# Transposes joined to values, score runs of a whole pair, and seven block products in two more MLP steps

## The chip, the cores and the metric

The kernel runs on one NeuronCore of a Trainium2 chip. The metric is device time in microseconds for one launch. A NeuronCore has a matmul engine (TensorE, PE in the profile, with its weight loads shown apart as PEld), VectorE (DVE), ScalarE (ACT), GpSimd (POOL) and a queue engine for transfers (SP). Matmul results land in PSUM, whose banks the kernel deals out by tags: two for `sc`, one each for `tr` and `xa`, and four shared ones.

## The reference

Two stages. The first is attention in chunks: batch 4, 8 heads, 768 rows, head size 64; each chunk of 32 rows sees 8 memory rows, its own 32 rows, 16 to the left and 8 to the right. The second takes the result as x (4 x 768 x 512), adds the real part of its 2D Fourier transform, normalizes rows, and adds a two-layer MLP.

```python
for c in range(nc):
    k_ctx, v_ctx = k[:, :, l_start:r_end], v[:, :, l_start:r_end]
    k_full = np.concatenate([mem_k, k_ctx], axis=2)
    v_full = np.concatenate([mem_v, v_ctx], axis=2)
    scores = scale * np.matmul(q_c, k_full.transpose(0, 1, 3, 2))
    a = softmax(scores)
    out[:, :, c_start:c_end] = np.matmul(a, v_full)
...
mixed = np.real(np.fft.fft(np.fft.fft(x, axis=1), axis=2))
u = x + mixed
un = (u - mu) / np.sqrt(var + 1e-06)
out = u + np.maximum(un @ w_ch1, 0.0) @ w_ch2
```

## The kernel before

**Attention.** Heads go in pairs, four pairs a batch, 16 pairs `n` in all (0 to 15). For pairs 0 to 11 q and k are loaded in natural order by POOL's queue (`e_load_qk`, three buffers each) and transposed by 16 small matmuls each (`e_turn_q` into the one PSUM bank of tag `tr`; `e_turn_k` into a shared bank for pairs 0 to 3, into `tr` for 4 to 11). ACT copies them out (`e_qT`, L423; `e_kT`, L448, by DVE for the first four pairs). For batch 3 (pairs 12 to 15) SP's DMA transposes do it instead. `e_scores` (L461) makes the scores of half a pair (12 matmuls of 64x64, six tiles of 64 rows for two heads) in the two banks of tag `sc`; `e_exp` (L469) takes them through exp on ACT in two instructions into one of three `e1` buffers; then the other half follows in the same two banks. From pair 4 on `e_values` (L485) runs for both halves in a row, 24 matmuls into the bank `xa` and 24 into a shared bank named `xo`. `e_norm` on DVE divides and writes to `xsb`.

**Fourier.** For each batch DVE folds the rows (`zy`, `pq`, `ff`, `lo`), ACT makes the upper halves of split numbers, PE multiplies with cosine and sine tables (`ps` L557, `pm` L727 and L608), DVE adds to `xsb` and takes statistics (L741, L742). Half of the mirrored rows comes back through DRAM (`x_rows`, `x_back`).

**MLP.** A batch has three steps `(b, j)` of 256 rows. `e_un` makes the normalized rows on ACT: in batches 0 and 1 it subtracts the mean alone, with the sign turned and `rstd` applied at the end; in batches 2 and 3 (the set `EVEN`) it applies scale and mean together, from `e_scale` on POOL. SP transposes them (`e_flip`, L776) into `unT`. Layer 1, `e_ch1` (L803): eight groups of 8 matmuls of 256 columns into a shared bank `ph`, each followed by a relu on ACT (L812) into `hT`. Layer 2 in batches 0 and 1: `e_ch2` (L821), 32 matmuls of 512 columns, and `e_res` (L828) on DVE. In the steps of the list `FAST`, so far those of batches 2 and 3, layer 2 is a 2 x 2 block product with seven block multiplications instead of eight: `e_prod` (L870), 56 matmuls of 256 columns; DVE prepares sums of the blocks of `hT` (`e_s`, L858) and adds the products to `xsb` (`e_add`, L875). The sums of weight blocks are made once (`e_w2t`, L845: four DVE instructions, the last of which overwrites a block of `w_sb` and so comes after the last plain layer 2).

**Shared banks.** Two banks of tag `acc` and two of tag `mlp`. `ph`, `pc`, `ps`, `pm` and `xo` live there; a task with a `pick` takes whichever of the four has been free longest.

**Order.** The order of all instructions on all engines is written out by a planner (`Plan`) when the kernel is built. Every task has an engine, a cost in microseconds, tasks it comes after, slots it takes and gives back, and a rank. `order` plays the list through in time: on each engine the task of lowest rank that is ready goes next; MLP matmuls have high ranks and fill PE's time between attention and Fourier tasks. `shortest` does this 24 times with the ranks of the later tasks shifted at random, and emits the order whose modelled end is earliest. The chip then runs each engine's queue in that order, with semaphores between engines.

Of the kernel before, what the change touches and what calls it, by code (L numbers as in the profile page):

```python
# [37 lines left out]
class Plan:  # L38
# [18 lines left out]
    def add(self, engine, cost, emit, after=(), take=(), give=(), rank=None, moved=0.0,  # L57
            loose=False, late=0.0, filler=False, behind=None, lag=0.0, pick=None, grain=0.1, head=1.0):
        t = dict(engine=engine, cost=cost, emit=emit, after=[a for a in after if a is not None],
                 take=take, give=give, rank=len(self.tasks) if rank is None else rank,  # L60
                 moved=moved, done=None, at=None, no=len(self.tasks), loose=loose,
                 late=late, filler=filler, behind=behind, lag=lag, pick=pick, grain=grain, head=head)
        self.tasks.append(t)
        return t
# [31 lines left out]
    def shortest(self, tries, spread):  # L96

        free, ranks = dict(self.free), [t["rank"] for t in self.tasks]
        found = None
        for i in list(range(tries)) + [None]:  # L100
            draw = random.Random(found[1] if i is None else i)
            even = (found[1] if i is None else i) == 0
            self.free = dict(free)
            for t, rank in zip(self.tasks, ranks):
                move = draw.gauss(0.0, spread)
                t["rank"] = rank if even or rank < self.lead or rank > 1e5 else rank + move
                t["done"] = t["at"] = None
                if t["pick"] is not None:
                    t["pick"].pop("tag", None)
            placed = self.order()  # L110
            if found is None or self.end < found[0]:
                found = (self.end, i)
        return placed

    def order(self):
# [9 lines left out]
        while any(waiting.values()):  # L125
# [5 lines left out]
            for e, ts_ in waiting.items():  # L131
# [3 lines left out]
                for t in ts_:  # L135
# [12 lines left out]
                    take = t["take"]  # L148
                    if t["pick"] is not None:
                        take += tuple(sorted((x for x in t["pick"]["of"] if self.free[x] > 0),  # L150
                                             key=lambda x: (since.get(x, []) + [0.0])[0]
                                             + t["pick"]["of"].index(x) * 0.5))[:1] or ("",)
                    for tag in take:
# [8 lines left out]
                    if t["pick"] is not None:  # L162
                        t["pick"]["tag"] = take[-1]
                    cost = t["cost"] * (2.0 if e == "PE" and now < self.WARM else 1.0)
# [41 lines left out]
def kernel(  # L206
# [15 lines left out]
    P = 128  # L222
# [217 lines left out]
    def e_kT(n, eng=None):  # L440
        if n >= TURNED * HP:
            win = LEFT + 64 + RIGHT
            nc.vector.tensor_copy(
                strided(kTb[n % NKT], MEM0 + NMEM, [[P, NT], [1, win]]),
                strided(kU[n % NKU], KR - LEFT, [[64, NT], [1, win]]))
            return
        trk = tr_of.pop((n, 1))
        (eng or nc.scalar.copy)(  # L448
            strided(kTb[n % NKT], MEM0 + NMEM, [[P, NT], [RB, 11], [1, RB]]),
            strided(trk, 0, [[64 // RB, NT], [1, 11], [KP, RB]]))  # L450
        if n < HP:
            let_go(trk)
# [284 lines left out]
    def e_stats(b, kt):  # L737
# [4 lines left out]
        nc.vector.bn_aggr(mu_of[b][:, kt, :], st6)  # L742

    def e_un(b, kt):
        un_of[b, kt] = un = fpool.tile([P, DM], FP16, tag="un", bufs=6, name="un")

        if b not in EVEN:
# [58 lines left out]
    def e_relu(b, j, i):  # L806
        if i == 0:
            shape = [P, 2, HH, 2 * P]
            hT_of[b, j] = (wpool.tile(shape, FP16, tag="w2t", bufs=1, name="hT") if (b, j) == (0, 1) else
                           fpool.tile(shape, FP16, tag="hT", bufs=1, name="hT"))  # L810
        ph = ph_of.pop((b, j, i))
        nc.scalar.activation(hT_of[b, j][:, :, i, :], ph, AFT.Relu, bias=0.0,  # L812
                             scale=1.0 if b in EVEN else -1.0)
        let_go(ph)
# [9 lines left out]
    def e_res(b, j, r):  # L824
        u, pc = xs[b][:, slot(b, 2 * j + r), :], pc_of.pop((b, j, r))
        st = slot(b, 2 * j + r)
        if b not in EVEN:
# [140 lines left out]

    t_used = {}

    def attention(n):
# [27 lines left out]
        else:  # L999
            tq = add("PE", 0.46, lambda: e_turn_q(n), [lq, t_idb], take=("tr",), give=("qs",))  # L1000
# [4 lines left out]
            tk = add("PE", 0.48, lambda: e_turn_k(n), [lk, t_idb, t_kz if n == 0 else t_kzs],  # L1005
                     take=(ktag,), give=("ks",))
            ek = add(dve[0], 1.25 if dve[1] else 1.04, lambda: e_kT(n, dve[1]), [tk, mk],
                     give=(ktag,))
        t_used[0, at], t_used[1, at] = (eq, tk) if b >= TURNED else (tq, tk)
        xs_ = []  # L1010
        for g in range(2):
            s_ = add("PE", 0.30, lambda g=g: e_scores(n, g), [eq, ek], take=("sc",),
                     give=("qT", "kTb") if g == 1 else (),
                     behind=t_sc.get((n, 0)))
            t_used["kTb", n % NKT] = s_
            t_sc[n, g] = s_
            t_exp[n, g] = x_ = add("ACT", 1.05, lambda g=g: e_exp(n, g),
                     [s_, t_masks, t_after.get(n)], take=("e1",), give=("sc",))
            xs_.append(x_)
# [191 lines left out]
    def columns_of(b, t_rest):  # L1211
# [31 lines left out]

        t_sum = {}
        columns(kts[0])
        for i, kt in enumerate(kts):
# [12 lines left out]
            sa = add("DVE", 0.9, lambda kt=kt: e_stats(b, kt), [su, sa])  # L1259
            if b in EVEN:  # L1260
                if i % 2:
                    t0, t1 = kts[i - 1], kt
                    sc_ = add("POOL", 1.7, lambda t0=t0, t1=t1: e_scale(b, t0, t1 - t0), [sa])
                    for t in (t0, t1):
                        un = add("ACT", 0.78, lambda t=t: e_un(b, t), [sc_], take=("un",))
                        t_un[t] = add("SP", 1.2, lambda t=t: e_flip(b, t), [un],
                                      behind=t_un.get(kts[kts.index(t) - 1]) if t else None,
                                      take=room(t), give=("un",), late=2.5, loose=True)
                continue
            un = add("ACT", 0.78, lambda kt=kt: e_un(b, kt), [sa], take=("un",))  # L1270
            if b > 0:
                t_un[kt] = add("SP", 1.2, lambda kt=kt: e_flip(b, kt), [un],
                               behind=t_un.get(kts[i - 1]) if i else None,
                               take=room(kt), give=("un",), late=2.5, loose=True)
# [4 lines left out]
                           take=room(kt), give=("mlp",))  # L1279
        return t_un, add("POOL", 2.05, lambda: e_rstd(b), [sa]) if b not in EVEN else None  # L1280

# [165 lines left out]
```

## Time and profile before

| | us |
|---|---|
| median of 3 runs | 280.53 (280.51 to 280.87) |
| the profiled execution | 280.87 |
| its span, first to last instruction | 279.2 |
| PE: starts of score runs, 32 of 12 matmuls | 13.0 to 182.5 |
| values of pairs 4 to 15 start at | 51.5, 59.7, 70.0, 81.4, 85.9, 90.9, 105.5, 112.2, 147.5, 152.8, 174.4, 185.5 |
| layer 1 of (1,0), (1,1), (1,2) starts at | 127.05, 151.8, 168.3 |
| last matmul starts | 275.7 |

A page of the profile covers one execution. Busy time of an engine is the union of its instructions. Matmuls overlap in their records, so how long a run of them holds TensorE is read from the distance between the start of the run and the start of the next. `x12` counts instructions merged into one line; `128*64 128x65` are weights and moving data. The granted TensorE clock is 1.00 in all stretches.

### The profile page before, as it was taken

What the parts mean: (1) busy time and instruction counts of PE and PEld (TensorE: products, weight loads), DVE (VectorE), ACT (ScalarE), POOL (GpSimd) and SP (SyncE); (2) the same over time, 40 slices, a digit from 0 to 9 for tenths busy, and PEclk for the clock granted to TensorE, in tenths of its full rate; (3) what the DMA queues carried; (4) which work ended last, traced back from release to release, by engine and by line L of the source; (5) the groups of instructions that cost most, each with busy time, mean ns of one, the idle gap of its engine ahead of it and who ended that gap; (6) DMA issues with size and microseconds to landing.
All of it is one profiled execution on the core that took longest, in us unless ns stands there. A gap on an engine that the chain in (4) does not pass through costs nothing.

```text
span 279.2 us, 7959 instructions
## 1 busy us (share of the span) xinstructions
PE 264.8 (95%) x3318; PEld 208.3 (75%) x3318; DVE 192.6 (69%) x424; ACT 154.7 (55%) x262; POOL 63.5 (23%) x127
## 2 busy tenths in 40 slices
PE   0599999999999999999999999999999999999995
PEld 0387797888765668758767857668889888888884
DVE  7968999941238999999937851259987975353444
ACT  6888647788777527636653556328164191605150
POOL 8852572330201096050211130001100130000000
PEclk9999999999999999999999999999999999999999
DMA  5998999999998999979992586824842057303152
GB/s 95 209 177 159 184 191 203 196 198 194 197 198 216 122 226 165 139 193 156 268 162 78 109 137 178 152 78 137 98 183 40 0 96 149 97 38 77 54 100 76
DMA packets 116116, 39.98 MB, mean 143 GB/s; under 512 B 104560, under 2 KB 111472, under 8 KB 116080
## 3 DMA queue, kind: packets, MB, share of 16 engines
q1 hardware_dynamic: 93888, 23.54, 45.6%
q0 software_dynamic: 21472, 15.21, 33.3%
q10 hardware_dynamic: 720, 0.72, 0.7%
q8 instruction: 26, 0.43, 0.7%
q14 instruction: 10, 0.08, 0.1%
HBM read 37.36 MB, written 13.37 MB: 182 GB/s over the span
## 4 chain that ended last, share of the span: by engine, by line
PE 82%; DVE 6%; POOL 5%; DMA 2%; ACT 2%; issue 2%; POOLq 0%; DVEq 0%
PE ph L803 26%; PE pc L821 15%; PE pc L870 11%; PE ps L557 6%; PE pm L727 5%; PE xa L485 4%; PE xo L485 4%; PE ps L716 3%; PE sc L461 3%; DMA qs<-in_q_dram 2%; PE trq L405 2%; PE trk L405 1%; PE idle L930 1%; ACT un L752 1%; PE pm L608 1%
## 5 line engine op out<-in xcount | busy, mean ns | idle before, releaser
L803 PE MATMUL ph<-unT,w_sb 128*128 128x256 f16 x768 | 90.0, 273 | 0.2 <-ACT hT L812 0.2
L812 ACT ACTIVATE hT<-ph 128x512 f16<-128x512 f32 x96 | 56.8, 597 | 47.3 <-PE ph L803 27.5
L803 PEld LDWEIGHTS <-w_sb 128*128 128x128 f16 x768 | 73.6, 98 | 10.8 <-issue 0.8
L821 PE MATMUL pc<-w_sb,hT 128*128 128x512 f16 x192 | 44.7, 380 | 0.0
L469 ACT ACTIVATE e<-sc,mbias 128x384 f32<-128x384 f32 x64 | 33.6, 580 | 17.7 <-PE sc L461 17.7
L821 PEld LDWEIGHTS <-hT 128*128 128x128 f16 x192 | 17.6, 98 | 19.2 <-issue 0.2
L870 PEld LDWEIGHTS <-hT 128*128 128x128 f16 x240 | 23.3, 98 | 3.9 <-issue 1.0
L875 DVE TENSOR_TENSOR xsb<-pc,xsb 128x256 f32<-128x256 f32 x43 | 17.8, 420 | 9.6 <-PE pc L870 8.4
L870 PE MATMUL pc<-w_sb,hT 128*128 128x256 f16 x192 | 24.1, 273 | 0.2 <-DVE xsb L875 0.2
L828 DVE SCALAR_TENSOR_TENSOR xsb<-pc,rstd,xsb 128x512 f32<-128x512 f32 x12 | 9.0, 749 | 18.8 <-PE pc L821 18.8
L569 ACT CAST up<-ps 128x386 f16<-128x386 f32 x16 | 9.7, 603 | 21.4 <-PE ps L557 20.4
L741 DVE BATCH_NORM_STATS2 st<-xsb 128x6 f32<-128x512 f32 x24 | 16.5, 687 | 0.5
L858 DVE TENSOR_TENSOR S<-hT 128x768 f16<-128x768 f16 (+1 forms) x12 | 5.1, 424 | 16.4 <-ACT hT L812 15.8
L485 PEld LDWEIGHTS xa<-va,e 128*64 128x64 f32 x384 | 13.1, 143 | 3.6 <-issue 2.9
L485 PE MATMUL xa<-va,e 128*64 128x65 f32 x384 | 15.4, 232 | 0.0
L752 ACT ACTIVATE un<-xsb,rs 128x512 f16<-128x512 f32 x12 | 9.5, 807 | 10.1 <-POOL rs L767 10.1
L485 PE MATMUL xo<-va,e 128*64 128x65 f32 x384 | 14.5, 227 | 0.0
L461 PEld LDWEIGHTS <-kTb 64*128 64x128 bf16 x384 | 7.7, 97 | 8.0 <-issue 5.3
L485 PEld LDWEIGHTS xo<-va,e 128*64 128x64 f32 x384 | 13.0, 142 | 0.4 <-ACT ff L651 0.3
L542 ACT CAST hi<-ff 128x768 f16<-128x768 f32 x12 | 9.9, 830 | 4.9 <-DVE ff L534 4.7
L461 PE MATMUL sc<-qT,kTb 64*128 64x64 bf16 x384 | 11.6, 196 | 0.9 <-POOL va L345 0.9
L870 PE MATMUL pc<-w_t,S 128*128 128x256 f16 x96 | 11.6, 272 | 0.4 <-DVE xsb L875 0.4
(168 smaller groups left out, 442.3 us busy)
## 6 DMA issues: line engine op xcount, KB each, us to landing
va<-in_v_dram SPq DMA_DIRECT2D x32, 220.0 KB
w_sb<-in_moe_w_ch_dram POOLq DMA_DIRECT2D x8, 512.0 KB, 14.5
out_dram<-xsb SPq DMA_DIRECT2D x12, 256.0 KB
qs<-in_q_dram POOLq DMA_DIRECT2D x12, 192.0 KB, 6.7
ks<-in_k_dram POOLq DMA_DIRECT2D x12, 192.0 KB, 6.7
x_rows<-xsb POOLq DMA_DIRECT2D x3, 768.0 KB, 4.6
xr<-x_back POOLq DMA_DIRECT2D x3, 768.0 KB, 6.0
out_rows<-xsb SPq DMA_DIRECT2D x9, 256.0 KB
```

The source lines that it names most:

```text
L461: nc.tensor.matmul(sc[:, hh, t6, :], kT[r0:r0 + 64, t, :], qT[r0:r0 + 64, ts(t, 64)], start=True, stop=True, tile_position=(r0, 0))
L469: nc.scalar.activation(e1[:, :, :, ts(half, 32)], sc[:, :, 0:6, ts(half, 32)], AFT.Exp, bias=mbias[:, half:half + 1], scale=1.0 / math.sqr ...
L485: nc.tensor.matmul(xa[64 * half:64 * half + 64, st, hh, 0:65], e1[:, hh, t6, :], v1[:, hh, 6 * g + t6, 0:65], start=True, stop=True)
L557: nc.tensor.matmul(out_[:, sp, :], part[:, ab, sp * 3 + st, c0:c1], tab[:, sp, st, :], start=(st == 0 and i == 0), stop=(st == 2 and i == 1))
L727: nc.tensor.matmul(pm[:, par, :], lhs, rhs[:, par, :], start=(im == 0), stop=(im == 3))
L741: nc.vector.bn_stats(st6, xs[b][:, kt, :])
L752: nc.scalar.activation(un, xs[b][:, kt, :], AFT.Identity, bias=rs[:, 1:2], scale=rs[:, 0:1])
L803: nc.tensor.matmul(ph[:, k, :], w1_sb[:, dt, ts(HH * k + i, P)], unT_of[b, j][:, dt, :], start=(dt == 0), stop=(dt == NDT - 1))
L812: nc.scalar.activation(hT_of[b, j][:, :, i, :], ph, AFT.Relu, bias=0.0, scale=1.0 if b in EVEN else -1.0)
L821: nc.tensor.matmul(pc_of[b, j, r], hT_of[b, j][:, k, i, ts(r, P)], w2_sb[:, HH * k + i, :], start=(i + k == 0), stop=(i + k == HH))
L870: nc.tensor.matmul(pc_of[key], a[:, i, :], w[:, i, :], start=(i == 0 and new), stop=(i == HH - 1), skip_group_check=not new)
L875: nc.vector.tensor_tensor(u, pc, u, ALU.add)
```

## The change

Four things, and the planner's costs that go with them.

1. A task can take more than one shared bank: `pick` becomes a list, `picks`.
2. `FAST` also holds (1, 1) and (1, 2). Tiles 1, 2, 4, 5 of batch 1 are therefore normalized with scale and mean together, in the two groups (1, 4) and (2, 5); tiles 0 and 3, of (1, 0), stay as they were. The sums of weight blocks now come after (1, 0).
3. For pairs 6 to 11 (`JOINED`) both transposes of pair n are emitted in the task of the values of pair n - 2, behind them; that task comes after the loads of pair n too, and takes `tr` for q and one more shared bank for k.
4. For pairs 8 to 15 all 24 score matmuls run in a row (`a_scores`), after the values of pair n - 1. The first six tiles go to `sc`, the other six to `tr` and to a shared bank, one for each head. `a_exp` takes the first half through exp in two instructions and the second in four.

The costs of single transposes, half score runs and values in the planner rise from 0.46, 0.48, 0.30 and 1.5 to 0.56, 0.56, 0.37 and 1.64; two transposes behind values add 0.81, and a run of a whole pair costs 0.52.

```diff
-    FAST = [(b, j) for b in range(2, B) for j in range(3)]
-    EVEN = {b for b, j in FAST}
+    FAST = [(1, 1), (1, 2)] + [(b, j) for b in range(2, B) for j in range(3)]
+    MIXED = 1
+    JOINED = set(range(HP + 2, TURNED * HP))
...
     def e_turn_k(n):
-        if n < HP:
-            trk = bank("acc", [P, RB * KP], BF16, "trk")
+        if n < HP or n in JOINED:
+            trk = bank("acc" if n < HP else pick_of["k", n]["tag"], [P, RB * KP], BF16, "trk")
...
+    def a_scores(n):
+        qT, kT = qT_of[n], kTb[n % NKT]
+        sc = aps.tile([P, 2, 8, 64], FP32, tag="sc", bufs=1, name="sc")
+        more = [aps.tile([P, 8, 64], FP32, tag="tr", bufs=1, name="sc2"),
+                bank(pick_of["s", n]["tag"], [P, 8, 64], FP32, "sc3")]
+        sc_of[n] = sc, more
+        for t in range(NT):
+            for hh in range(2):
+                r0 = 64 * hh
+                nc.tensor.matmul(sc[:, hh, t, :] if t < 6 else more[hh][:, t - 6, :],
+                                 kT[r0:r0 + 64, t, :], qT[r0:r0 + 64, ts(t, 64)],
+                                 start=True, stop=True, tile_position=(r0, 0))
+
+    def a_exp(n, g):
+        sc, more = sc_of[n]
+        e1_of[n, g] = e1 = apool.tile([P, 2, 6, 64], FP32, tag="e1", bufs=3, name="e1")
+        for half in range(2):
+            for to, src in [(e1, sc[:, :, 0:6])] if g == 0 else [(e1[:, i], more[i][:, 0:6]) for i in range(2)]:
+                last = len(to.shape) - 1
+                cut = (slice(None),) * last + (ts(half, 32),)
+                nc.scalar.activation(to[cut], src[cut], AFT.Exp, bias=mbias[:, half:half + 1],
+                                     scale=1.0 / math.sqrt(D))
+        if g == 1:
+            let_go(more[1])
...
+    def even(b, kt):
+        return (b, SLOT.index(kt) // 2) in FAST
...
+            if n in JOINED:
+                tk, ktag = tq, pick_of.setdefault(("k", n), dict(of=("mlp", "acc")))
+                tk["after"] += [lq, lk]
+                tk["cost"] += 0.81
+                tk["take"] += ("tr",)
+                tk["give"] += ("qs", "ks")
+                tk["picks"].append(ktag)
...
+        whole = n >= 8
+        if whole:
+            sp_ = pick_of["s", n] = dict(of=("mlp", "acc"))
+            s_ = add("PE", 0.52, lambda: a_scores(n), [eq, ek, t_val[n - 1]], take=("sc", "tr"), pick=sp_, give=("qT", "kTb"))
...
-                v_ = add("PE", 1.5, lambda: [e_values(n, i) for i in range(2)],
+                v_ = t_val[n] = add("PE", 1.64, lambda: [e_values(n, i) for i in range(2)]
+                                    + [x(n + 2) for x in (e_turn_q, e_turn_k) if n + 2 in JOINED],
                          xs_ + [lv, t_low[n % NV]], take=("xa",), pick=vp, give=("e1", "e1", "va"))
...
-            if b in EVEN:
+            if b > MIXED or b == MIXED and even(b, kt):
+                if kt == 1 and b == MIXED:
+                    continue
                 if i % 2:
-                    t0, t1 = kts[i - 1], kt
+                    t0, t1 = kts[i - 1] if b > MIXED or kt == 5 else 1, kt
                     sc_ = add("POOL", 1.7, lambda t0=t0, t1=t1: e_scale(b, t0, t1 - t0), [sa])
```

More of the change, by code (lines that the diff above doesn't have):

```diff
@@ L61, in add @@
                  moved=moved, done=None, at=None, no=len(self.tasks), loose=loose,
[L62 removed]
+                 late=late, filler=filler, behind=behind, lag=lag, picks=[pick] if pick else [], grain=grain, head=head)
         self.tasks.append(t)
@@ L107, in shortest @@
                 t["done"] = t["at"] = None
-                if t["pick"] is not None:
-                    t["pick"].pop("tag", None)
+                for pick in t["picks"]:
+                    pick.pop("tag", None)
             placed = self.order()
@@ L148, in order @@
                     take = t["take"]
-                    if t["pick"] is not None:
-                        take += tuple(sorted((x for x in t["pick"]["of"] if self.free[x] > 0),
+                    for pick in t["picks"]:
+                        got = take[len(t["take"]):]
+                        take += tuple(sorted((x for x in pick["of"] if self.free[x] > got.count(x)),
                                              key=lambda x: (since.get(x, []) + [0.0])[0]
-                                             + t["pick"]["of"].index(x) * 0.5))[:1] or ("",)
+                                             + pick["of"].index(x) * 0.5))[:1] or ("",)
                     for tag in take:
@@ L161, in order @@
                             since[tag].pop(0)
-                    if t["pick"] is not None:
-                        t["pick"]["tag"] = take[-1]
+                    for pick, tag in zip(t["picks"], take[len(t["take"]):]):
+                        pick["tag"] = tag
                     cost = t["cost"] * (2.0 if e == "PE" and now < self.WARM else 1.0)
@@ L999, in attention @@
         else:
-            tq = add("PE", 0.46, lambda: e_turn_q(n), [lq, t_idb], take=("tr",), give=("qs",))
+            tq = (add("PE", 0.46 if first else 0.56, lambda: e_turn_q(n), [lq, t_idb], take=("tr",), give=("qs",))
+                  if n not in JOINED else t_val[n - 2])
             dve = ("DVE", nc.vector.tensor_copy) if n < HP else ("ACT", None)
@@ L1004, in attention @@
             ktag = "acc" if first else "tr"
-            tk = add("PE", 0.48, lambda: e_turn_k(n), [lk, t_idb, t_kz if n == 0 else t_kzs],
-                     take=(ktag,), give=("ks",))
+            if n in JOINED:
[5 more added lines that the diff above has]
+                tk["picks"].append(ktag)
+            else:
+                tk = add("PE", 0.48 if first else 0.56, lambda: e_turn_k(n), [lk, t_idb, t_kz if n == 0 else t_kzs],
+                         take=(ktag,), give=("ks",))
             ek = add(dve[0], 1.25 if dve[1] else 1.04, lambda: e_kT(n, dve[1]), [tk, mk],
@@ L1010, in attention @@
         xs_ = []
+        whole = n >= 8
+        if whole:
+            sp_ = pick_of["s", n] = dict(of=("mlp", "acc"))
+            s_ = add("PE", 0.52, lambda: a_scores(n), [eq, ek, t_val[n - 1]], take=("sc", "tr"), pick=sp_, give=("qT", "kTb"))
         for g in range(2):
[L1012 to L1019, printed above, removed]
+            if whole:
+                t_used["kTb", n % NKT] = t_sc[n, g] = s_
+                t_exp[n, g] = x_ = add("ACT", 1.05 if g == 0 else 1.55, lambda g=g: a_exp(n, g),
+                                       [s_, t_masks, t_after.get(n)] + xs_, take=("e1",),
+                                       give=("sc",) if g == 0 else ("tr", sp_))
+                xs_.append(x_)
+            else:
+                s_ = add("PE", 0.30 if first else 0.37, lambda g=g: e_scores(n, g), [eq, ek], take=("sc",),
+                         give=("qT", "kTb") if g == 1 else (),
+                         behind=t_sc.get((n, 0)))
+                t_used["kTb", n % NKT] = s_
+                t_sc[n, g] = s_
+                t_exp[n, g] = x_ = add("ACT", 1.05, lambda g=g: e_exp(n, g),
+                         [s_, t_masks, t_after.get(n)], take=("e1",), give=("sc",))
+                xs_.append(x_)
             if not first and g == 0:
@@ L1265, in columns_of @@
                         un = add("ACT", 0.78, lambda t=t: e_un(b, t), [sc_], take=("un",))
-                        t_un[t] = add("SP", 1.2, lambda t=t: e_flip(b, t), [un],
-                                      behind=t_un.get(kts[kts.index(t) - 1]) if t else None,
+                        t_un[t] = t_one = add("SP", 1.2, lambda t=t: e_flip(b, t), [un],
+                                      behind=t_one,
                                       take=room(t), give=("un",), late=2.5, loose=True)
@@ L1271, in columns_of @@
             if b > 0:
-                t_un[kt] = add("SP", 1.2, lambda kt=kt: e_flip(b, kt), [un],
-                               behind=t_un.get(kts[i - 1]) if i else None,
+                t_un[kt] = t_one = add("SP", 1.2, lambda kt=kt: e_flip(b, kt), [un],
+                               behind=t_one,
                                take=room(kt), give=("un",), late=2.5, loose=True)
@@ L1279, in columns_of @@
                            take=room(kt), give=("mlp",))
-        return t_un, add("POOL", 2.05, lambda: e_rstd(b), [sa]) if b not in EVEN else None
+        return t_un, add("POOL", 2.05, lambda: e_rstd(b), [sa]) if b <= MIXED else None
     mlp_prev, t_sums, side_end = [None], [], []
```

12 lines of the change are left out of this document (6 added, 6 removed).

## The prediction

> **What bounds the kernel now.** I read the page's busy shares first, then its 40 slices, then the busy time in stretches, then TensorE's instructions in order of time, and last the waits.
>
> ```profile
> PE 264.8 (95%) x3318; PEld 208.3 (75%) x3318; DVE 192.6 (69%) x424; ACT 154.7 (55%) x262; POOL 63.5 (23%) x127
> ...
> PE   0599999999999999999999999999999999999995
> ...
> DVE  7968999941238999999937851259987975353444
> ACT  6888647788777527636653556328164191605150
> ```
>
> PE is full from the third slice to the last but one. After the start DVE is full only in slices 13 to 20 and nearly so in 28 to 33, ACT nowhere for long. The stretches (TensorE, weight loads, DVE, ACT, POOL, clock, DMA) say the same in microseconds:
>
> ```profile
> 50.00:84.00 34.00, 34.00 (x622) 26.74 (x619) 13.99 (x38) 26.36 (x45) 6.76 (x10) 1.00 1.18 197
> 84.00:112.00 28.00, 28.00 (x411) 19.73 (x409) 26.14 (x47) 15.84 (x27) 11.46 (x14) 1.00 1.24 184
> 112.00:140.00 28.00, 27.77 (x257) 20.63 (x254) 26.83 (x50) 16.35 (x26) 5.74 (x7) 1.00 1.23 187
> 140.00:186.00 46.00, 46.00 (x517) 30.85 (x516) 20.33 (x46) 22.75 (x40) 5.49 (x13) 1.00 0.63 128
> ```
>
> From 33 us to the end of its work TensorE waits for other engines only 0.8 us in the list of waits, 0.2 for a relu (L812) and 0.6 for a residual add (L875). So the time is the sum of the distances from one TensorE start to the next, and an edit is worth what it takes from that sum unless it opens a gap. The distances are in the timeline (start, length, instruction, count):
>
> ```profile
> 64.32 0.35 PE L461 MATMUL sc<-qT,kTb 64*128 64x64 bf16 x12
> 64.60 1.92 PE L803 MATMUL ph<-unT,w_sb 128*128 128x256 f16 x16
> 66.45 0.35 PE L461 MATMUL sc<-qT,kTb 64*128 64x64 bf16 x12
> 66.73 1.92 PE L803 MATMUL ph<-unT,w_sb 128*128 128x256 f16 x16
> 68.58 0.53 PE L405 MATMUL trq<-ident_b,qs 96*64 96x96 bf16 x16
> 69.05 1.05 PE L803 MATMUL ph<-unT,w_sb 128*128 128x256 f16 x8
> 70.02 0.92 PE L485 MATMUL xa<-va,e 128*64 128x65 f32 x24
> 70.77 0.87 PE L485 MATMUL xo<-va,e 128*64 128x65 f32 x24
> 71.47 0.53 PE L405 MATMUL trk<-turn_b,ks 100*64 100x100 bf16 x16
> 71.93 1.92 PE L803 MATMUL ph<-unT,w_sb 128*128 128x256 f16 x16
> ```
>
> Eight ph matmuls followed by more of the MLP take 0.875 us to the next start (57.62 to 58.50), so 16 take 1.75; here 16 take 1.85 ahead of scores and ahead of transposes, and 8 take 0.97 ahead of values. **A change of matmul shape costs 0.10 us** before the attention work. Behind values the same shows: xo takes 0.80 when MLP or scores follow (153.51 to 154.31), 0.70 when transposes follow (70.77 to 71.47).
>
> **Scores in one run, pairs 8 to 15.** A run of 12 takes 0.28 us to the next start. Its records span 0.35 and the last one is 0.19 long, so the 12 starts lie within 0.16, 14.5 ns apart; the remaining 0.12 is a tail. Two runs cost 2 x (0.28 + 0.10) = 0.76; one run of 24 costs 23 x 0.0145 + 0.12 + 0.10 = 0.55. That saves 0.21, over eight pairs **1.7 us**. No run of 24 is in this trace. If a run's cost is proportional to its count (24 x 23 ns = 0.56) only the entry is saved, 8 x 0.10 = 0.8; if the second half came at no tail and full overlap it could not save more than 8 x 0.38 = 3.0. I take 1.7, which follows from the start distances inside a run. On ACT the second half of a pair's exps becomes four of 128x192 instead of two of 128x384. No exp of that width is in the trace; the shortest ACT instructions here take 0.20 us and the pair of 128x384 takes 1.05, so the four cost between 1.05 and 1.85. I take 1.5: +0.5 a pair, 4 us in all, behind ACT's 46 - 22.75 = 23 us idle in the stretch 140 to 186 and 12 in 84 to 112. Without that cover each 0.5 would delay the relu queued behind it.
>
> **Transposes behind older pairs' values, pairs 6 to 11.** What the twelve runs cost now, with the 0.10 where they follow MLP and without it where they follow scores or values: q 0.46, 0.57, 0.46, 0.56, 0.47, 0.47; k 0.35, 0.36, 0.57, 0.48, 0.48, 0.58; sum 5.81. After: 16 starts lie 21.6 ns apart (0.53 less the last one's 0.206, over 15), a lone run takes 0.47, so its tail is 0.14 and 32 in a row take 31 x 0.0216 + 0.14 = 0.81. Values then take 1.45 instead of 1.55, so a block adds 0.71, six add 4.26: saved **1.55 us**, or 0.83 if cost were proportional to count (6 x 0.83 = 4.98). The same 24 q and k loads are issued on POOL, tied now to the values: values of pair 4 wait for loads of pair 6 (q issued at 36.5, landed 13.2 later; k 37.2 plus 13.8: 51.0, and the values ran at 51.54), those of pair 5 for pair 7 (46.4 + 19.3 and 49.0 + 17.9, so 66.9 instead of 59.69). Behind that wait stand DVE's normalizing of pair 5, the v load of pair 9 on SP, and the loads of pair 10 on POOL, whose buffers the transposes free. Against it, the transposes of k for pair 7 come at 67 instead of 71.5, and pair 9's k load need not wait for a transpose at 61.1 any more.
>
> **Seven block products for (1,1) and (1,2).** Plain and blocked layer 2 in the timeline:
>
> ```profile
> 161.39 7.07 PE L821 MATMUL pc<-w_sb,hT 128*128 128x512 f16 x32
> ...
> 243.00 1.91 PE L870 MATMUL pc<-w_sb,hT 128*128 128x256 f16 x16
> 244.74 1.91 PE L870 MATMUL pc<-w_t,S 128*128 128x256 f16 x16
> 246.66 1.03 PE L870 MATMUL pc<-w_sb,hT 128*128 128x256 f16 x8
> 247.54 1.04 PE L870 MATMUL pc<-w_t,hT 128*128 128x256 f16 x8
> 248.41 1.04 PE L803 MATMUL ph<-unT,w_sb 128*128 128x256 f16 x8
> ```
>
> 32 x 0.216 = 6.91 us (161.39 to 168.30) against 56 x 0.109 = 6.11 plus the 0.17 by which 244.74 to 246.66 exceeds 1.74, the wait for a residual add. Saved 0.64 a block, **1.3 us** for two (0.8 if each waits 0.41 like the first one at 197.23; 1.6 without any). The Trainium skill (TensorE: Matmul & The Clock Gate, "Back-to-back issue gap") gives a sustained spacing of about 131 ns for 512 columns, by which a plain layer 2 would take about 4.2 us as an estimate and the blocks would lose. This trace has 216 ns at 512 columns and 109 at 256, and I go by that.
>
> Per block DVE gains S passes (3 x 0.56 + 3 x 0.29 + 0.68 = 3.2) and 7 adds of 0.42, and loses two residuals of 0.75: +4.6, two blocks +9.3, against 25.7 us idle DVE in 140 to 186. The last weight sum (1.21) moves from 186.3, where DVE is full, to the end of (1,0), near 152. POOL gets two scale groups of 1.6 us (as 149.97 to 151.6) in the in-order queue ahead of x_rows at 121.97; un of tiles 1, 4, 2, 5 comes some 2 us later, and (1,1) starts only at 152. All free as long as these covers hold; gone, they'd cost the 2 us at (1,1)'s start.
>
> **Sum.** -1.7 - 1.55 - 1.3 = -4.5. New waits: 14 places now take one more shared PSUM bank (six k transposes, eight score runs). Bounds: nothing, and one whole ph (0.87) each, 12 us. Nearest row: twelve value blocks already take such a bank, and all waits of ph for a relu are 0.23 us. I take 0.4. Net -4.1. The profiled execution took 280.87 (span 279.2 and 1.7 around it), so it would be 276.8; its median stands 0.34 lower, at 280.53, which gives **276.4**, with 275.2 to 277.5 as this case's own range.
>
> **Rivals.**
>
> *Cost follows the count, not the runs.* Then transposes save 0.83 and scores 0.8: -2.9 + 0.4, 278.0. For it: no doubled run at full clock is in the trace. Against it: the starts inside a run are 14.5 ns apart, not 23. Chance 0.10.
>
> *Batch 1 becomes late.* Values of pair 5 are held 7.2 us. If the whole batch moved by that, its first flips, on SP until 119.8 and ready perhaps at 121, would be ready at 128; (1,0) starts at 127.05 now, and 2.4 us earlier after the savings up to there (1.55 + 4 x 0.21). PE would idle 3.5 us: 279.9. Against it: the last values (81.35) hang on pair 7's transposes, which get earlier. DVE at 26 of 28 us from 84 on can't make up lateness. Chance 0.11.
>
> *Shared banks and ACT, slower.* A block with transposes holds two of the four shared banks (xo, trk), and the copies qT (0.79) and kTb (1.04) stand ahead of relus on ACT. Two banks left let one ph run on (0.87), and ACT has 0.28 spare between relus: PE waits 1.83 - 0.87 - 0.28 = 0.68, six times 4.1. Score runs: the added 0.5 of exps less 0.28, eight times 1.8. Together 5.9 against 4.5: **281.9**. It decides from 0.32 us a place on. For it: from 50 to 84 ACT is at 26.4 of 34 us. Against it: about a third of the stretch 50 to 186 is layer 1 (48 x 0.875 of 136); elsewhere pc matmuls need no new bank. The Trainium skill (TensorEngine Tiling (Array Packing), "PSUM Bottleneck") warns of just this: tiled matmuls get faster, emptying PSUM does not. Chance 0.21.
>
> **How the numbers follow.** Forecast 0.58, the rivals 0.10, 0.11, 0.21. A measurement of this kernel tells about 0.2% (0.6 us) from no change. Faster: 0.58 + 0.10 + 0.07 of the late batch = 0.75; same 0.04; slower 0.21. The range goes from 274.9 (no waits, and 1.1 more than counted) to 281.4, which leaves out the upper half of the slow rival.
>
> **What would show it.** Right: sc in runs of 24 taking 0.45 to the next start; trq and trk back to back at 0.81; 112 more pc matmuls of 256 columns and 64 fewer of 512; no wait of PE over 0.5 us between 50 and 230. Wrong: ph waiting for hT or e above 3 us in total; PE waiting for unT or for q and k loads; the values of pair 7 later than 83.

## The result, and the profile after

| | before | after |
|---|---|---|
| median of 16 runs each, in turn on one chip (us) | 280.72 (280.26 to 281.41) | 278.31 (277.14 to 281.27) |
| ratio after to before [95% interval] | | 0.9919 [0.9903, 0.9936] |
| the profiled execution (us) | 280.87 | 281.27 |
| its span (us) | 279.2 | 279.4 |

The kernel became faster by 2.4 us; the forecast was 4.1 faster, 276.4 us, with the range up to 281.4. The 278.31 lies outside the 275.2 to 277.5 that the prediction gave for its own mechanism; it lies in the wide range, which takes in the rivals' times. Two things about the table matter for what follows. The runs after spread over 4.1 us, those before over 1.2. And the execution that was profiled is the slowest of the 16, so its page must not be read as the typical one; a second profile of the same kernel (e13 below, 277.50 us) stands beside it.

The page of the changed kernel, first the busy time by engine, then the 40 slices:

```profile
PE 262.0 (94%) x3365; PEld 213.5 (76%) x3365; DVE 201.0 (72%) x448; ACT 156.4 (56%) x278; POOL 66.7 (24%) x135
...
PE   0599999999999989999999699999999999999995
...
PEclk9999999999999999999999799999999999999999
```

The covers are about as large as worked out. POOL has 3.2 us more, twice the 1.6 of a scale group. ACT has 1.7 more where 4 were expected. DVE has 8.4 more where 9.3 were expected. TensorE has a new hole in slice 23 (154 to 161 us), and in the same slice the granted clock is down. Two of the stretches that the prediction showed, and a short one behind the hole (columns as there):

```profile
84.00:112.00 28.00, 27.24 (x429) 20.84 (x424) 26.04 (x45) 20.42 (x39) 9.81 (x12) 1.00 1.15 200
140.00:186.00 46.00, 43.18 (x525) 35.34 (x522) 29.72 (x71) 22.08 (x45) 5.24 (x13) 0.96 0.82 132
156.43:159.84 3.41, 3.41 (x19) 2.35 (x17) 3.24 (x10) 0.60 (x1) 1.19 (x4) 0.50 1.06 119
```

TensorE lost 0.8 us in 84 to 112 and 2.8 in 140 to 186, where it had lost nothing before, and after the second hole it ran for 3.4 us at half of its clock. The timeline says where (start, length, instruction, count, idle time before it and what ended it):

```profile
86.50 0.52 PE L484 MATMUL sc<-qT,kTb 64*128 64x64 bf16 x24
86.96 3.63 PE L851 MATMUL pc<-w_sb,hT 128*128 128x512 f16 x16
90.51 0.92 PE L512 MATMUL xa<-va,e 128*64 128x65 f32 x24
91.26 0.87 PE L512 MATMUL xo<-va,e 128*64 128x65 f32 x24
91.96 0.51 PE L407 MATMUL trq<-ident_b,qs 96*64 96x96 bf16 x16
92.31 0.53 PE L407 MATMUL trk<-turn_b,ks 100*64 100x100 bf16 x16
92.76 1.04 PE L851 MATMUL pc<-w_sb,hT 128*128 128x512 f16 x4
...
98.24 1.05 PE L833 MATMUL ph<-unT,w_sb 128*128 128x256 f16 x8
99.65 1.91 PE L833 MATMUL ph<-unT,w_sb 128*128 128x256 f16 x16 [0.36 <-DVE up L601]
101.95 1.03 PE L833 MATMUL ph<-unT,w_sb 128*128 128x256 f16 x8 [0.40 <-ACT e L495]
...
155.97 0.39 PE L754 MATMUL pm<-cosD,up 128*128 128x256 f16 x2 [2.81 <-DVE xsb L644]
...
157.25 6.67 PE L833 MATMUL ph<-unT,w_sb 128*128 128x256 f16 x48
163.76 1.91 PE L900 MATMUL pc<-w_sb,hT 128*128 128x256 f16 x16
165.51 1.91 PE L900 MATMUL pc<-w_t,S 128*128 128x256 f16 x16
167.43 1.03 PE L900 MATMUL pc<-w_sb,hT 128*128 128x256 f16 x8
168.30 1.04 PE L900 MATMUL pc<-w_t,hT 128*128 128x256 f16 x8
169.27 0.52 PE L484 MATMUL sc<-qT,kTb 64*128 64x64 bf16 x24
...
196.34 2.19 PE L900 MATMUL pc<-w_t,S 128*128 128x256 f16 x16
...
233.64 1.03 PE L900 MATMUL pc<-w_sb,hT 128*128 128x256 f16 x8 [0.16 <-DVE xsb L905]
```

The work itself is as priced. A run of 24 scores takes 0.46 to the next start (86.50 to 86.96); 0.45 was forecast. The two transposes take 0.35 + 0.45 = 0.80 (91.96 to 92.76); 0.81 was forecast. Of the 56 matmuls of (1,1) 48 are the four lines from 163.76: 1.75, 1.92, 0.87, and 0.97 ahead of scores.

What the waits cost is more than their brackets say. Eight ph take 0.875 to the next start when nothing waits; from 98.24 to 99.65 it is 1.41, so 0.53 were lost and 0.36 are shown. The last record of a run reaches some 0.17 past the moment at which the next could have started, and a wait is shown from there on. A small wait isn't shown at all: one of 0.29 lies inside the run at 196.34, whose length is 2.19 instead of 1.91, and one of 0.32, at 233.64, shows as 0.16.

Two of the three large waits are of the kind that the prediction priced at 0.4 in all: the one at 99.65 is for the bank of a Fourier product, which DVE reads (L601), and the one at 101.95 for the exps of the second half of a score run, which hold its shared bank. ACT's timeline of the same execution explains it:

```profile
99.33 0.60 ACT L842 ACTIVATE hT<-ph 128x512 f16<-128x512 f32 x1
99.82 0.82 ACT L569 CAST hi<-ff 128x768 f16<-128x768 f32 x1
100.54 1.36 ACT L495 ACTIVATE e<-sc,mbias 128x192 f32<-128x192 f32 x4
```

The second half's four exps stand behind a relu and a Fourier cast, so the shared bank taken at 97.72 comes free at 101.90. The third wait (2.81) is of another kind, which no step of the prediction had.

### The mirrored rows of batch 2

The third `pm` of batch 2 (L754) waits for a bank that `e_sum_back` (L642, L644) empties; that adds the mirrored rows `xr`, which come back from DRAM. The chain that ended last, from 140 to 165 us of the changed kernel, shows it (start, us, what):

```profile
134.53 7.53 SPq L623
...
145.84 9.29 DMA xr<-x_back
155.13 0.02 issue
155.16 0.69 DVE xsb L642
155.85 0.08 DVE xsb L644
155.92 0.05 issue
155.97 1.48 PE pm L754 x8
```

Before, `xr` was issued at 142.99, landed 6.8 us later at 149.8, and DVE used it first at 155.82: 6 us of slack.

```profile
142.99 0.75 POOL L600 DMA_DIRECT2D xr<-x_back x1 [8.96 <-DMA x_back<-x_rows]
...
155.82 0.68 DVE L615 TENSOR_TENSOR xsb<-pm,xr 128x510 f32<-128x510 f32 x1
```

Now the work ahead of it ends earlier (DVE was ready for it at 152.26), while the rows come later. In the four profiled executions of the changed order that read them (e4 with one edge more):

| execution | `xr` issued | to landing | PE waits | time |
|---|---|---|---|---|
| the changed kernel, first profile | 145.84 | 9.3 | 2.81 | 281.27 |
| e1, again | 145.2 | 7.6 | 0.45 | 278.45 |
| e4, one more edge | 145.4 | 7.0 | 0.33 | 277.98 |
| e13, again | 144.4 | 6.9 | none | 277.50 |

In the slowest one the 2.81 was not all: by start distances the wait is 2.97, the eight pm after the wait took 1.28 to the next start instead of 0.875, and the 48 ph 6.51 instead of 5.25, at the lowered clock. That is 1.7 more. 281.27 - 2.97 - 1.7 = 276.6.

Why the rows come later is seen in part. POOL's `x_rows` went from 121.97 to 126.94, behind the two scale groups and `rstd`, which waited for `un`; but SP's `x_back` starts at 133.34 as before (133.30), since it stands behind transposes of q and k and output transfers. Its larger part takes 7.53 instead of 6.36, and the v load of pair 15, at 158.2 before, is now issued from 148.5 on, beside `xr`. That load can't be the whole cause: in e13 it is issued at 148.35, beside `xr` too, and `xr` takes 6.9, as before.

### The profile page after: what moved, and what is told of

Read it like the earlier page. It is cut to its first block, busy times and chain, and to the rows that moved or that the text cites. A ratio compares the mean times of both kernels' runs of the same rounds, so it can differ in the third digit from the quotient of the medians.

```text
span 279.4 us, 8093 instructions
## 1 busy us (share of the span) xinstructions
PE 262.0 (94%) x3365; PEld 213.5 (76%) x3365; DVE 201.0 (72%) x448; ACT 156.4 (56%) x278; POOL 66.7 (24%) x135
## 4 chain that ended last, share of the span: by engine, by line
PE 62%; DVE 16%; DMA 5%; POOL 5%; SPq 4%; ACT 4%; issue 2%; POOLq 0%; DVEq 0%; ACTq 0%
PE ph L833 24%; PE pc L900 16%; PE pc L851 5%; PE ps L584 4%; PE pm L754 4%; DMA xr<-x_back 3%; SPq L623 3%; PE xa L512 2%; PE xo L512 2%; DMA qs<-in_q_dram 2%; DVE xsb L523 2%; DVE ff L665 1%; ACT hT L842 1%; DVE st L768 1%; PE trq L407 1%
## 5 line engine op out<-in xcount | busy, mean ns | idle before, releaser
L905 DVE TENSOR_TENSOR xsb<-pc,xsb 128x256 f32<-128x256 f32 x57 | 23.8, 422 | 13.6 <-PE pc L900 12.0
L900 PE MATMUL pc<-w_sb,hT 128*128 128x256 f16 x256 | 32.0, 273 | 0.2 <-DVE xsb L905 0.2
L851 PE MATMUL pc<-w_sb,hT 128*128 128x512 f16 x128 | 29.8, 380 | 0.0
L495 ACT ACTIVATE e<-sc,mbias 128x192 f32<-128x192 f32 (+1 forms) x48 | 18.6, 482 | 8.4 <-PE sc L484 8.4
L471 ACT ACTIVATE e<-sc,mbias 128x384 f32<-128x384 f32 x32 | 16.8, 576 | 4.6 <-PE sc L463 4.2
L782 ACT ACTIVATE un<-xsb,rs 128x512 f16<-128x512 f32 x16 | 12.4, 805 | 10.3 <-POOL rs L797 10.3
L900 PE MATMUL pc<-w_t,S 128*128 128x256 f16 x128 | 15.6, 273 | 0.1
L900 PEld LDWEIGHTS <-S 128*128 128x128 f16 x128 | 12.4, 98 | 1.8 <-issue 0.3
L425 ACT COPY qT<-trq 128x768 bf16<-128x768 bf16 x12 | 9.5, 795 | 7.3 <-PE trq L407 7.3
L754 PEld LDWEIGHTS <-up 128*128 128x128 f16 x96 | 9.2, 99 | 4.9 <-DVE xsb L644 3.1
```

The lines of the kernel that those rows point to most:

```text
L495: nc.scalar.activation(to[cut], src[cut], AFT.Exp, bias=mbias[:, half:half + 1], scale=1.0 / math.sqrt(D))
L754: nc.tensor.matmul(pm[:, par, :], lhs, rhs[:, par, :], start=(im == 0), stop=(im == 3))
L851: nc.tensor.matmul(pc_of[b, j, r], hT_of[b, j][:, k, i, ts(r, P)], w2_sb[:, HH * k + i, :], start=(i + k == 0), stop=(i + k == HH))
L900: nc.tensor.matmul(pc_of[key], a[:, i, :], w[:, i, :], start=(i == 0 and new), stop=(i == HH - 1), skip_group_check=not new)
```

## The experiments

All are versions of the changed kernel. Each is compared with the kernel before on the same chip; where the text has "the distance", it is that from the start of the first Fourier matmul of batch 0 (31.6 to 33.1 us) to the last matmul's start, in the profiled execution; it holds the same matmuls in all kernels but for the edits. Executions of the changed kernel alone differ by 0.7 us (31.59 to 32.30) in where that first start falls.

**The same again, and without the wait for the mirrored rows.** The first theory was that the wait for `xr` is what the gain lost. Its rival: many small waits. e2 lets batch 2 add its own rows where the mirrored ones belong, so that nothing waits for `xr`.

> The changed kernel once more, for a second profile on the chip of the next three. Mirror theory (TensorE stands at the third pm of batch 2 until the mirrored rows xr land, and runs at a lower granted clock afterwards; that is what keeps the gain at 2.4 instead of 4.1): the wait before pm at 153 to 156 us is there again, with another length than 2.8, and this execution's time less that wait and less the slow stretch behind it is 276.5 to 277. Shared-bank theory: waits of ph for relus and exps sum to over 2 us. Size theory (the edits save less than counted): no single wait above 1 us and the time still 278.

```diff
-        r = xr[:, kt, :].rearrange("p (j c) -> p c j", c=2)
+        r = y if b == 2 else xr[:, kt, :].rearrange("p (j c) -> p c j", c=2)
```

> Same order of all instructions; for batch 2 the mirrored half adds its own rows instead of xr, so nothing waits for xr (that batch's mirrored rows are not the reference's; xr is still loaded). Mirror theory: the wait at the third pm goes, no stretch of lower clock, 276.2 to 277.0, all executions close together. Shared-bank and size theories: 278 as before, since neither has to do with xr.

Measured: e1 277.66 (277.39 to 278.45), ratio 0.9887 [0.9865, 0.9909]; e2 277.74 (277.36 to 278.37), 0.9887 [0.9866, 0.9909]. The two are the same. So the theory fell for the typical execution; it holds for the profiled one of the first 16 (281.27). Of the others only 280.51 shows a lowered mean clock (0.994) as that one does, and e1's four executions have none like it. What is left of the waits in e2 (the list of TensorE's waits after the start):

```profile
PE pc L900 <- DVE xsb L905: 0.6, 2, 0.4
PE ph L833 <- ACT e L495: 0.4, 1, 0.4
PE ph L833 <- DVE up L601: 0.4, 1, 0.4
PE ph L833 <- ACT hT L842: 0.3, 1, 0.3
```

**Telling the planner that the rows are late, and holding the v load behind them.** e3 lets the planner take `xr` as landing 4 us later, with the ranks kept those of the changed kernel; it then puts three more ph groups ahead of the third `pm`. e4 puts the v load of pair 15 behind the issue of `xr`.

```diff
-        t_xr[b] = add("POOL", 1.0, lambda: e_mirror(b), [t_x2[b]], take=("dn",), moved=2.0, grain=0.16)
+        t_xr[b] = add("POOL", 1.0, lambda: e_mirror(b), [t_x2[b]], take=("dn",), moved=2.0, grain=0.16, late=4.0)
```

> The planner is told that xr lands 4 us later than it thought, the random ranks being those of the changed kernel; three more groups of ph then stand ahead of the third pm of batch 2 on TensorE, the transfers on POOL keep their order. Mirror theory: the wait is covered by those 2.6 us of ph, 276.3 to 277.3. Shared-bank theory: more ph with fewer free banks, no gain, 278 or above. Size theory: 278.

```diff
     t_lv[15]["behind"] = t_x2[TURNED - 1]
+    t_lv[15]["after"].append(t_xr[TURNED - 1])
```

> The v load of pair 15 is put behind the load of xr, the random ranks being those of the changed kernel; two transfers on SP change places. If xr is slow to land (9.3 us against 6.8 before) because the v load shares the transfer engines with it: xr lands in about 7 us, the wait shrinks from 2.8 to about 0.5, time 276.8 to 277.6. If xr is late mainly because the rows went out late (POOL at 126.9 instead of 122.0): the wait stays, 278.

Measured: e3 282.97 (282.5 to 283.46), 1.0072 [1.0051, 1.0093], the slowest of all; e4 277.98 (277.1 to 279.4), 0.9899 [0.9867, 0.9932]. e4 settles nothing: no faster, a spread of 2.3, and 0.33 of the wait left. Nor did its edit keep the two transfers apart: the v load is issued at 149.38, 0.9 later than in the first profile, and `xr` lands at 152.36. e3 is 5.3 slower than e1 for a wait of 0.45 to be filled. Its own waits:

```profile
PE ph L833 <- ACT hT L842: 1.2, 1, 1.2
...
PE pm L754 <- DVE xsb L644: 0.7, 1, 0.7
```

Ten recorded waits after 33 us in place of e1's six, 5.0 us instead of 2.2. The `pm` wait of 0.7 is that of another batch, at 219.3. Filling that place with layer 1 takes the groups from where they covered something else, and the largest wait (1.2 at 157.6) is for a relu that stands on ACT behind two normalizations, which waited 0.9 for POOL's scale group. The fill costs more than the hole.

**The parts, alone and together.** e5 leaves `FAST` as it was before, e6 leaves out the joined transposes and the whole score runs, e7 and e8 have one of these alone, e9 has none of the three edits and keeps only the planner's new costs.

```diff
-    FAST = [(1, 1), (1, 2)] + [(b, j) for b in range(2, B) for j in range(3)]
+    FAST = [(b, j) for b in range(2, B) for j in range(3)]
```

```diff
-    JOINED = set(range(HP + 2, TURNED * HP))
+    JOINED = set()
...
-        whole = n >= 8
+        whole = False
```

e5 has the first diff, e6 the second; e7 the first and `whole = False`, e8 the first and the empty `JOINED`, e9 all.

> Joined transposes and whole score runs, without the two new block-product steps. Size theory as counted: 3.25 us less TensorE work than before. If the missing 1.4 us are waits of the block products for their adds (pc for xsb, 0.4 and 0.4 with what lies hidden under the records), this kernel has only the two waits of ph near 100 us and comes to 280.7 - 3.25 + 0.8 = 278.2. If the joined blocks and score runs are what costs (shared banks), it comes to 279 or more.

> The two block-product steps alone. As counted, 1.6 us less TensorE work without waits; with a wait of 0.17 to 0.43 for an add in each, 0.9 to 1.3: 279.4 to 279.8. If DVE, which gets 9.3 us more, or the later normalization is the cost, TensorE idles for unT, hT or S and the time is 280.5 or more.

> The joined transposes alone. Run theory: six tails of 0.14 and 7 or so shape changes of 0.10 saved, 1.55 us, so 279.1 if no new wait comes; the kernel shows trq and trk 0.34 and 0.46 apart in six places. Rival (batch 1 late because pair 5's values wait for pair 7's loads): the values of pair 7 start after 83 and TensorE waits for unT of (1,0); 280 or more.

> The whole score runs alone, pairs 8 to 15. Run theory: 0.21 a pair, 1.7 us: 279.0 without new waits. Bank theory: the run holds one more shared bank until six exps are through (2.3 us), and that is what ph waited for at 102; with one or two such waits of 0.5 the time is 279.5 to 280, with more of them 280.5 or above.

> None of the three edits, only the planner's higher costs for single transposes, half score runs and values, so the order of the kernel before is drawn anew from the same work. If orders are worth little: 280.3 to 281.2, and the parts alone can be read against the kernel before. If the order drawn decides as much as an edit: off by more than 0.8 us either way, and 282.0 for the block products alone says nothing about block products.

| | median | ratio | distance, less the 243.4 before | of it waits | of it work | work, as the prediction counts it |
|---|---|---|---|---|---|---|
| e9 costs only | 280.91 | 1.0004 [0.9990, 1.0018] | 0.0 | +0.1 | -0.1 | 0 |
| e8 scores only | 279.50 | 0.9951 [0.9935, 0.9967] | -0.9 | +0.7 | -1.6 | -1.7 |
| e7 transposes only | 280.31 | 0.9982 [0.9964, 1.0000] | +0.6 | +2.4 | -1.8 | -1.55 |
| e6 products only | 282.03 | 1.0038 [1.0013, 1.0063] | +1.3 | +3.1 | -1.8 | -1.6 |
| e5 scores and transposes | 278.54 | 0.9915 [0.9896, 0.9934] | -1.6 | +1.6 | -3.2 | -3.25 |
| e1, all | 277.66 | 0.9887 [0.9865, 0.9909] | -2.6 | +2.4 | -4.9 | -4.85 |

Waits and work are told apart by start distances. Between two matmuls of the same two kinds they repeat in all these traces (0.109 us between two of 256 columns, 0.205 from one of these to a score); what a distance has over its usual value is counted as wait, from 0.04 us on, and the rest as work. The kernel before has 2.1 us of waits by this count, where the list of its waits shows 0.8. The last column has the products without the waits that the prediction counted into them.

The parts don't add. Alone they bring -1.4, -0.5 and +1.1 us, together -3.2 on e1's chip; the products cost time alone. Whether they save any beside the others is not shown: e5 and e1 have overlapping intervals, and the first 16 runs of the whole change (0.9919) are no faster than e5. The columns of waits and work say why the parts don't add: the work falls by about what was counted in every kernel, but each kernel has an order of its own, and each order has waits of its own. In e6 the blocked layer 2 catches up with a relu and with the adds:

```profile
166.98 0.50 PE L900 MATMUL pc<-w_sb,hT 128*128 128x256 f16 x3 [0.90 <-ACT hT L842]
```

In e7 it is the rival "Batch 1 becomes late", which the changed kernel does not show: (1,0) waits for its flips, at the place and near the time (127 to 128) that the rival named, for 1.8 where it had 3.5 (that profiled execution, 281.34, is 1.0 above e7's median):

```profile
127.47 3.76 PE L833 MATMUL ph<-unT,w_sb 128*128 128x256 f16 x33 [1.77 <-DMA unT<-un]
```

Since e9 equals before, the costs by themselves cause nothing that shows. The waits rest on one execution each, and I trust them to about 0.5.

**The order alone.** e10 takes the planner's second-best order; e12 searches 160 orders instead of 24, with `xr` taken as 2 us late and the narrow exps at 1.3 instead of 1.55, nearer to what they measured; e13 is the changed kernel beside it.

```diff
-        for i in list(range(tries)) + [None]:
+        for i in [4, None]:
```

> The whole change, in the order that the planner ranks second of its 24 (it models it 0.8 us longer). Same instructions. If TensorE's saved work (4.6 us by count) is what the time follows, 277.5 to 278.8. If order decides, waits of TensorE differ by more than 1.5 us from the 2.2 of the changed kernel and the time goes with them.

```diff
-                t_exp[n, g] = x_ = add("ACT", 1.05 if g == 0 else 1.55, lambda g=g: a_exp(n, g),
+                t_exp[n, g] = x_ = add("ACT", 1.05 if g == 0 else 1.3, lambda g=g: a_exp(n, g),
...
-        t_xr[b] = add("POOL", 1.0, lambda: e_mirror(b), [t_x2[b]], take=("dn",), moved=2.0, grain=0.16)
+        t_xr[b] = add("POOL", 1.0, lambda: e_mirror(b), [t_x2[b]], take=("dn",), moved=2.0, grain=0.16, late=2.0)
...
-        for t in plan.shortest(24, 1.5):
+        for t in plan.shortest(160, 1.5):
```

> The whole change with a planner that tries 160 orders instead of 24, takes xr to land 2 us later and the four narrow exps to cost 1.3 instead of 1.55. If the remaining 1.4 us over the forecast are waits, which a better order avoids: 276.4 to 277.4. If the waits that come on the chip aren't in the planner's model, 277.5 to 278.5, as the changed kernel beside it.

> The changed kernel once more on the chip of the kernel with 160 orders, for comparison: 277.4 to 278.4, waits of TensorE after 33 us of 1.6 to 3.7 in its records, the two of ph near 99.7 and 102 among them in any case, since they hang on banks and exps and on no transfer.

Measured: e10 278.50 (278.21 to 280.34), 0.9922 [0.9894, 0.9950]; e12 278.46 (277.81 to 278.96), 0.9915 [0.9890, 0.9940]; e13 277.56 (277.47 to 278.11), 0.9891 [0.9869, 0.9912]. Two other orders of the same work are 0.8 to 0.9 us slower than the one the change has in e1 and e13, by their medians; the intervals overlap, and the first 16 runs of the change have about the same ratio (0.9919), so a difference is not shown. By start distances e10's work is that of e1 (-4.9), and so are its waits (+2.3). Its largest are of banks, which DVE empties after it has waited 0.36 for `xr`:

```profile
PE ph L833 <- DVE xsb L644: 1.7, 2, 1.2
```

In e12's profiled execution TensorE stops for 2 us in the middle of a score run:

```profile
105.95 0.44 PE L484 MATMUL sc<-qT,kTb 64*128 64x64 bf16 x18
108.34 0.26 PE L484 MATMUL sc<-qT,kTb 64*128 64x64 bf16 x6 [1.96 <-issue]
```

The view names nothing that it waited for, and no other profile here has such a stop. Without its 2.1 us e12's waits would be +0.9, fewer than e1's, and the 278.90 of this execution would be 276.8. So e12 does not show that its order is worse; what the stop is, and whether e12's other executions have it, stays open. e13's profile, in the block that the first profile showed disturbed:

```profile
153.57 1.91 PE L833 MATMUL ph<-unT,w_sb 128*128 128x256 f16 x16
155.76 3.65 PE L833 MATMUL ph<-unT,w_sb 128*128 128x256 f16 x32 [0.28 <-ACT hT L842]
159.25 1.91 PE L900 MATMUL pc<-w_sb,hT 128*128 128x256 f16 x16
161.00 2.15 PE L900 MATMUL pc<-w_t,S 128*128 128x256 f16 x16
163.58 1.03 PE L900 MATMUL pc<-w_sb,hT 128*128 128x256 f16 x8 [0.43 <-DVE xsb L905]
```

No wait for `xr`, but 2.19 instead of 1.75 at 153.57 and 2.58 instead of 1.75 at 161.00. The 0.83 are two waits for adds: 0.25 inside the run of 16, which is 2.15 long instead of 1.91 and has no bracket, and 0.59 where the bracket shows 0.43.

## Why the prediction came out as it did

**What bounds the kernel.** Right: TensorE's distances are the time, before and after. From the first Fourier matmul on they sum to 243.4 before, and to 240.5 (e13), 240.8 (e1) and 240.2 (e2) after.

**Scores, 1.7.** Right: e8, which has the whole score runs alone, saves 1.6 of work. In e13 the start distances of all score runs after 33 us sum to 5.97 against 6.78, and five fewer changes into scores (14 instead of 19) at 0.10 add 0.5. Scores and transposes together, in e5, save 3.2 where 3.25 was forecast. The narrow exp was taken too high: 0.434 us each, and the whole pair's six 2.29, +0.2 a pair instead of +0.5.

**Transposes, 1.55.** Right in size; e7, which has them alone, saves 1.8 of work. The reading of what they would hold back was off: the values of pair 4, which were worked out to stay at 51.5, started at 61.0, since the q load of pair 6, issued at 38.49, landed only at 57.99. The values of pair 5 were held to 69.86, further than the 66.9 worked out, and those of pair 7 started at 82.42, inside the bound of 83; (1,0) did not become late in this kernel.

**Products, 1.3.** The work is as priced: (1,1) took 6.28 and (1,2) 6.14 in the first profile against 6.91, and e6, which has them alone, saves 1.8 of work. But in e13, where TensorE had not stood still just before, (1,1) has 0.84 of waits for its adds and gains nothing. The trace agrees with a spacing of 109 ns at 256 columns, and the term was taken from that.

**"I take 0.4."** Here it failed: a term of the sum was mis-sized. The work saved is 4.9 us in e1, e2 and e13, as against 4.85 counted. The distances fell by 2.6 (e1), 2.9 (e13) and 3.2 (e2, with no wait for `xr`). So 2.4, 2.1 and 1.7 us came back as waits, where the prediction had 0.4 and, inside the products, 0.34. In e13 they are, by start distances: the two ph on shared banks near 99 and 102 us with 0.5 each, a `pm` at 44.1 that waits for its operand `up` with 0.5 (0.15 before), the relu at 155.76 with 0.45, and the products' adds with 0.84. Two large waits of the kernel before went, 0.4 and 0.6 by start distances:

```profile
118.40 1.91 PE L803 MATMUL ph<-unT,w_sb 128*128 128x256 f16 x16 [0.23 <-ACT hT L812]
...
197.23 1.03 PE L870 MATMUL pc<-w_t,S 128*128 128x256 f16 x8 [0.41 <-DVE xsb L875]
```

The bounds given, 0 and 12, held it; the choice leaned on "all waits of ph for a relu are 0.23 us", which counted the brackets (each some 0.17 too low) and took it that a new order would wait little more than the one before. The runs say otherwise: but for e9, which keeps the work, every version has 0.7 us of waits or more beyond those before. That less work leaves less to fill gaps with would explain it; that is argued, not shown.

**"Free as long as these covers hold."** POOL's cover did hold for `x_back`, though `x_rows` came 5.0 later. What was not priced is the other side: `xr` had 6 us of slack, and in the first profile it landed 5.3 later and was wanted 3.6 sooner. That cost nothing in e13, 0.5 to 0.6 in e1 and e4, and 4.6 in the first profile, lowered clock included. It may make part of the spread of the first 16 runs, but it does not explain their median: without the two executions of lowered clock that is still 278.25. So of the 1.9 us between forecast and result some 1.2 go with the waits beyond the forecast (2.1 in e13 where 0.74 was counted), and the 0.7 between the first 16 runs (278.31) and e1 and e13 (277.6) stays open.

**Rivals.** "Cost follows the count" gave 278.0, nearest to the median, by luck: 24 scores take 0.46 and not 0.56, 32 transposes 0.80 and not 0.94. "Batch 1 becomes late" appeared in e7 alone (its sum has a slip: 128 less 124.65 is 3.35, not 3.5). "Shared banks and ACT, slower" has its mechanism at one of its 14 places, the exps at 101.95, with the wait at 99.65 beside it, at about 0.5 each; it needed 0.32 on average at all of them.

**What would show it.** The signs for sizes came. "No wait of PE over 0.5 us between 50 and 230" held for e1, e2 and e13 by the brackets alone (by start distances each has waits of 0.5 to 0.6), and the 2.81 in the first profile broke it.

**Left open.** Why `xr` takes 6.9 us in one execution and 9.3 in another was not settled. A third buffer for the scale groups and `rstd`, which would let `x_rows` go out sooner, gave no time (e11): the pool then needs 58.53 KB a partition in SBUF, and 58.47 are left.

## What to carry to other kernels

Where one engine is full and an order is planned, price the work by start distances, and then allow for waits that the new order brings: here 1.7 to 2.4 of 4.9 us saved came back. Look up the slack of every transfer that returns to the full engine's path, and subtract the gain ahead of it: 6 us of slack was gone after an edit that named no transfer. Parts measured alone don't add up to the whole: here they gave -1.4, -0.5 and +1.1 us, and -3.2 together.

## What the runs showed of the hardware

After the wait of 2.81 us the granted clock stood at 0.50 for 3.41 us (156.43 to 159.84), and cost another 1.7; after e7's wait of 1.77 and e12's stop of 1.96 it stayed at 1.00. The Trainium skill (TensorE: Matmul & The Clock Gate, "Part 1: The HAM clock gate") says that the clock falls to half after an idle window of about 3.4 us and comes back after as long a busy one. The half and the 3.41 us agree with it; the gap that went before it here, 2.81 us, was shorter than the page's window.

A change of matmul shape, taken as 0.10 us from the trace before, holds in the trace after as well: eight pc matmuls take 0.97 us to the next start ahead of scores (168.30 to 169.27) and 0.87 ahead of more of their kind (167.43 to 168.30). The Trainium skill (TensorEngine Tiling (Array Packing), "Key Properties") says that changing the tiling mode drains TensorE, without a price.
